# Attention into a GELU MLP on one core: four added exps per key in the first and last pair, products with v ahead of the sums, the last store in parts

## The chip, the cores and the metric

The kernel runs on one core of a Trainium2 chip. A core has five engines with instruction queues of their own: TensorE (PE; its weight loads are a row of their own, PEld), VectorE (DVE), ScalarE (ACT), GpSimd (POOL) and SyncE (SP, which here only issues DMAs). The metric is the device time of one execution in microseconds (us), and lower is better.

## The reference

Attention with normed queries and keys over 8 batches of 12 heads, 448 tokens and 64 channels; the heads are put side by side, and the 3584 tokens of 768 channels go through an MLP of width 2048:

```
q_n, k_n = rmsnorm(q, g_q), rmsnorm(k, g_k)
scores = matmul(q_n, k_n.T) / sqrt(64)
attn   = exp(scores - max); attn = attn / (sum(attn) + 1e-9)
x      = concat_heads(matmul(attn, v))          # 3584 x 768
out    = gelu_tanh(x @ w_in) @ w_out            # 768 -> 2048 -> 768
```

## The kernel before

**Work of one batch.** Batches are counted from 0 to 7. The twelve heads of a batch are six pairs (`hp` 0 to 5). The 448 keys stand in four key tiles of 112 (`kt`). `scores` (L208) multiplies one key tile of a pair with all queries: two matmuls, one per head, on separate halves of TensorE's rows, into a PSUM tile `sc` of which there are two; ScalarE takes the exp of both heads in one instruction (L218) into `ex`. `key_sums` (L222) lets VectorE add key tiles 0 and 1, then 2 and 3, into `es` (two additions per pair, batches 2 to 7 only; in batches 0 and 1 it returns). `pair_sums` (L231) is called twice per pair. With `what` 0 it sums over the keys: matmuls of `ones` with `es` (two key halves, two heads, so four matmuls) into the PSUM tile `o0`; then VectorE turns the sums into reciprocals that are spread over the channels: a transpose `st` (L253), a reciprocal `rc` (L254), a transpose `rb` (L255). With `what` 1 it multiplies `ex` with v (eight matmuls) into `o1`, and VectorE multiplies `o1` with `rb` into `xT` (L248). The two heads' matmuls stand in separate halves of TensorE's columns.

**Order of the work.** The order on every engine is written out by hand (`manual_schedule`, L62): each engine runs its instructions in the order of the Python code, and waits where data or a buffer is missing. The loop at L549 does for each batch b: the first MLP product `mm1` (L259; 16 tiles of six matmuls, each followed by a gelu on ScalarE), between whose tiles `m1` puts other work by slots; then `attention(b + 1)` (L334), between whose parts it puts the second MLP product `mm2` (L273) of earlier tokens: 112 steps of one matmul (96 in the first), given out by `upto`. Sixteen steps make half the columns of a tile of 128 tokens, and a copy by VectorE (L294) takes that out of PSUM; the PSUM tiles of `mm1` and `mm2` share a pool of two (`ps_m`). Within a pair the order on TensorE is: scores of key tiles 0 and 1, two steps of `mm2` in column halves, the previous pair's sums and products, scores of key tiles 2 and 3, nine or ten steps of `mm2`. The first pair has 20 and 30 as its counts (`first`), and ahead of and behind the last pair's sums stand 17 and 7 steps (`last`, L337).

**The next batches.** For batch b+1 GpSimd multiplies the loaded q and k with their inverse norms (L159, twelve instructions, slot 0 of `m1`), SP transposes them by DMA into `qT` and `kT` (L199), and VectorE multiplies `kT` with the gains (L204). For batch b+2 SP loads q and k (L96), ScalarE and, for the last third of the heads, GpSimd square them (L121, L123), and VectorE totals the squares (L128). The totals of that last third stand in slots 1 and 2 of the attention's `side`, on VectorE's queue between the first pair's two additions; the inverse norms are taken in slot 11 (L137, L140).

**The end.** Behind the last `mm1` stand 128 steps of `mm2`. Each tile of 128 tokens is stored when its second half is copied, in two DMAs on SP (L301), since its tokens cross a border of the output's layout. In this last stretch ScalarE copies the first halves (L292) and VectorE the second ones.

Of the kernel before, what the change touches and what calls it, by code (L numbers as in the profile page):

```python
# [8 lines left out]
F32 = mybir.dt.float32  # L9
BF16 = mybir.dt.bfloat16  # L10
# [6 lines left out]
def kernel(  # L17
# [11 lines left out]
    nc = tc.nc  # L29
    B, H, S, D = q.shape  # L30
    assert (B, H, S, D) == (8, 12, 448, 64)
    d_model = H * D
# [4 lines left out]
    HP = H // 2  # L37
# [87 lines left out]
    def total(b, c, n, hs=slice(0, CH)):  # L125
        if b not in sss:
            sss[b] = smp.tile([P, NCH, 2, CH, NK], F32, tag="ss", name="ss")
        nc.vector.reduce_sum(  # L128
            sss[b][:, c, "qk".index(n), hs], sqs[n, b, c][:, hs], axis=AX.X
        )  # L130
# [90 lines left out]

    def key_sums(b, hp, i):  # L222

        if b < 2:
            return
        if i == 0:
            ess[b, hp] = exq.tile([P, 2, 2, S], BF16, tag="es", name="es")
        ex = exs[b, hp]
        nc.vector.tensor_add(ess[b, hp][:, i], ex[:, 2 * i], ex[:, 2 * i + 1])  # L229

    def pair_sums(b, hp, what, waits=0):  # L231


        o = oas[what] = ps_o.tile([128, S], F32, tag=f"o{what}", name=f"o{what}")
        idle(waits, o)

        e = exs[b, hp] if what or b < 2 else ess[b, hp]
        n = e.shape[1]
        for i in range(n):
            for a in range(2):  # L240
                nc.tensor.matmul(  # L241
                    o[a * D:(a + 1) * D], vb[b % 2][:, 2 * hp + a, i] if what else ones, e[:, i, a],
                    start=(i == 0), stop=(i == n - 1),
                )
        if what:
            if hp == 0:
                xT[b] = xp.tile([128, HP, S], BF16, tag="xT", name="xT")
            nc.vector.tensor_mul(xT[b][:, hp], o, oas["rb"])  # L248
            return
        st = stp.tile([128, S // 32, 32], F32, tag="st", name="st")  # L250
        oas["rb"] = stp.tile([128, S], F32, tag="rb", name="rb")
        rc = smp.tile([128, S // 32], F32, tag="rc", name="rc")
        nc.vector.transpose(st.rearrange("p a b -> p (a b)"), o)  # L253
        nc.vector.reciprocal(rc, st[:, :, 0])  # L254
        nc.vector.transpose(oas["rb"], rc.to_broadcast([128, S // 32, 32]))  # L255

    hs1 = {}

# [14 lines left out]
    def mm2(b, i, half, f, parts=1):  # L273


        if f == 0:
            osbs["ps"] = ps_m.tile([128, 512], F32, tag="mm", name="o")
            if half == 0:
                osbs[i] = op.tile([128, d_model], F32, tag="osb", name="osb")
        o, osb = osbs["ps"], osbs[i]  # L280
        m = 128 // parts
        for j in range(parts):
            nc.tensor.matmul(  # L283
                o[j * m:(j + 1) * m, :HD], g[:, f, i * 128 + j * m:i * 128 + (j + 1) * m],
                wout[:, f, half * HD:(half + 1) * HD],
                start=(f == 0), stop=(f == nf - 1),
            )
        if f + 1 < nf:
            return
        part = osb[:, half * HD:(half + 1) * HD]  # L290
        if b + 1 == B and half == 0:
            nc.scalar.copy(part, o[:, :HD])  # L292
        else:
            nc.vector.tensor_copy(part, o[:, :HD])  # L294
        if half == 1:
            j = i * 128
            while j < (i + 1) * 128:
                bb, t, p = j // S, j % S // P, j % P
                m = min(P - p, (i + 1) * 128 - j)
                r = ((b // 2) * 2 + bb) * P + p  # L300
                nc.sync.dma_start(  # L301
                    out_v[t, r:r + m], osb[j - i * 128:j - i * 128 + m]
                )
                j += m

    def mm1_pair(i, cs=range(HP)):
# [27 lines left out]
    def attention(b, m2, quota, side):  # L334


        first, last, even = (20, 30), (17, 7), 2 if b > 1 else 0  # L337
        given = 0

        def upto(k, parts=1):  # L340
            nonlocal given
            while given < k:
                m2.pop(0)(parts)
                given += 1

        spread = quota - first[1] - sum(last)
        for hp in range(HP):
            for odd in range(2):
                i = 2 * hp + odd
                for fn in side.get(i, ()):  # L350
                    fn()
                if hp and not odd:
                    key_sums(b, hp - 1, 1)
                for kt in range(2 * odd, 2 * odd + 2):
                    scores(b, hp, kt)
                if not hp:
                    upto(first[odd])
                elif odd:
                    upto(first[1] + spread * hp // (HP - 1))
                else:  # L360

                    upto(given + even, 2)
                    for what in range(2):
                        pair_sums(b, hp - 1, what)
                if not odd:
                    key_sums(b, hp, 0)
        key_sums(b, HP - 1, 1)
        nc.scalar.preload_act_table_set(GELU_SET)
        upto(given + last[0])
        for what in range(2):  # L370
            pair_sums(b, HP - 1, what)
        upto(quota)

    def first_attention(side, mid, early, late):
# [128 lines left out]
    load_v(0, 6, 6)  # L503
    total(0, 1, "q", slice(0, 2))

    def pool_waits(b, c, n, j):

        nc.gpsimd.tensor_copy(mark, nrms[n, b, c][:1, j, 0, 0, :1])

    side = [(1, lambda: normed0(1, nc.vector), lambda: pool_waits(0, 0, "k", 1),  # L510
             lambda: squares0(3, nc.gpsimd), lambda: total(0, 1, "k", slice(0, 2)),
# [37 lines left out]
    for b in range(B):  # L549
        m1, side = [], []  # L550
        if b == 0:
            m1 = [(1, lambda: normed1(0), lambda: total(1, 1, "q"), lambda: total(1, 1, "k"),
                   lambda: load_v(1, CH, 2 * CH), lambda: rsqrt_pow(1, 1),
                   lambda: normed_all(1, 1)),
                  (2, lambda: total(1, 2, "q"), lambda: total(1, 2, "k"),
                   lambda: rsqrt_pow(1, 2), lambda: normed_all(1, 2)),
                  (3, lambda: trans(1, 0, ps_m)),
                  (4, lambda: trans(1, 1, ps_m), lambda: transposed(1, 1)),
                  (5, lambda: loads(2, 0), lambda: loads(2, 1)), (6, lambda: loads(2, 2))]
            side += [(0, lambda: transposed(1, 2)),  # L560
                     (2, lambda: gain(1, 1)), (5, lambda: gain(1, 2))]

            for c, slots in enumerate(((3, 5), (7, 9), (10, 11))):
                for n, slot in zip("qk", slots):
                    side += [(2 * c + 1, lambda c=c, n=n: square(2, c, n, nc.gpsimd)),
                             (slot, lambda c=c, n=n: total(2, c, n))]
        elif b + 1 < B:
            for c in range(NCH):
                m1 += [(0, lambda c=c: normed_all(b + 1, c)),
                       (4 * c + 4, lambda c=c: transposed(b + 1, c))]  # L570
            m1 += [(9, lambda: gain(b + 1, 0)), (14, lambda: gain(b + 1, 1))]
            side.append((3, lambda: gain(b + 1, 2)))
        if 0 < b and b + 2 < B:
            m1 += [(4, lambda: loads(b + 2, 1)), (8, lambda: loads(b + 2, 2))]
            for c, at in ((0, 1), (1, 9)):
                for i, (n, half) in enumerate((n, half) for n in "qk" for half in range(2)):
                    m1.append((at + i, lambda c=c, n=n, half=half: squared(b + 2, c, n, half)))
                m1 += [(at + 2, lambda c=c: total(b + 2, c, "q")),
                       (at + 4, lambda c=c: total(b + 2, c, "k"))]
            for n, slot in (("q", 1), ("k", 2)):  # L580
                m1.append((13, lambda n=n: square(b + 2, 2, n, nc.gpsimd)))
                side.append((slot, lambda n=n: total(b + 2, 2, n)))
        m1 = plan(*m1)
        for f in range(nf // 2 if b == 0 else nf):
            if b > 0:
                mm1(b, f)
            elif f > 1:
                mm1_pair(f)
            for fn in m1.get(f, ()):
                fn()  # L590
        m2 += m2_parts(b)
        if b + 1 == B:
            for fn in m2:
                fn()
            break
        nc.scalar.preload_act_table_set(EXP_SET)  # L596
        if b + 2 < B:
            side += [(11, lambda: rsqrt(b + 2)),
                     (0, lambda: load_v(b + 2, 0, H))]
            if b + 3 < B:  # L600
                side.append((1, lambda: loads(b + 3, 0)))
        attention(b + 1, m2, 96 if b == 0 else 112, plan(*side))


# [28 lines left out]
```

## Time and profile before

| what | value |
|---|---|
| median of 3 runs (lowest, highest) | 451.08 us (450.93, 451.17) |
| the profiled execution's own time | 451.04 us |
| span in its profile | 449.3 us |
| granted TensorE clock, mean | 0.996 |
| busy share: PE, ACT, DVE, POOL | 96%, 68%, 56%, 38% |
| one `mm1` of a batch, in the chain | 18.17 us |
| attention of batch 4, from its first scores to the next `mm1` | 217.83 to 251.05 us |
| start of the last copy; the last store's two issues on SP | 444.46; 445.09 to 445.87 us |

Times of single instructions are us from the start of the span. A timeline line gives the start, the stretch, engine, line, operation and how many instructions it merges; in brackets stands the idle time of the engine ahead of it and what ended that. A matmul's own duration (about 0.35 us) is longer than the distance to the next one, since matmuls overlap; distances between starts are used here. The profiled execution took 1.74 us more than its span, which no view splits up.

### The profile page before, as it was taken

The page shows a single profiled execution, that of the slowest core. Times are in us where ns is not written, and L with a number is a line of the kernel's source. Part 1 is how long each engine was busy: PE and PEld are TensorE (multiplying, and loading weights), DVE is VectorE, ACT ScalarE, POOL GpSimd, SP SyncE. Part 2 cuts the span into 40 slices and gives each one's busy share as a digit, 9 for nine tenths or more (in the row PEclk, how much of TensorE's full clock was granted, in tenths as well). Part 3 has the DMA queues.
Part 4 walks back from the last instruction along what each step waited for, and adds up shares of the span by engine and source line. Part 5 has one row for each costly group of instructions (what it writes and reads, how often), then busy time and mean ns, then how long its engine had stood idle before and what let it go on. Part 6 is the DMA issues. An engine that isn't in the chain of part 4 may idle for free.

```text
span 449.3 us, 7158 instructions
## 1 busy us (share of the span) xinstructions
PE 432.5 (96%) x2835; PEld 217.4 (48%) x2835; DVE 251.9 (56%) x426; ACT 303.7 (68%) x404; POOL 168.8 (38%) x142
## 2 busy tenths in 40 slices
PE   8889998899999999999999999999999999999995
PEld 3334543355445554455545544455544554545563
DVE  5889423943687428862588437872398513871000
ACT  5995477557787578857889468856888348863400
POOL 5997894573303740083402921064400900000000
PEclk9999999899999999999999999999999999999999
DMA  8999999159911939119911868118841511111022
GB/s 226 257 232 213 204 247 224 48 118 238 181 35 42 231 88 179 35 54 251 190 41 36 190 133 174 42 36 205 138 77 35 120 41 36 36 36 36 0 72 70
DMA packets 80754, 54.47 MB, mean 121 GB/s; under 512 B 39248, under 2 KB 75600, under 8 KB 80720
## 3 DMA queue, kind: packets, MB, share of 16 engines
q1 hardware_dynamic: 63936, 42.22, 38.5%
q0 software_dynamic: 16624, 11.80, 17.9%
q8 instruction: 22, 0.36, 0.3%
q14 instruction: 12, 0.10, 0.1%
q10 hardware_dynamic: 160, 0.00, 0.0%
HBM read 45.61 MB, written 11.01 MB: 126 GB/s over the span
## 4 chain that ended last, share of the span: by engine, by line
PE 70%; POOL 12%; DVE 7%; ACT 4%; DMA 4%; issue 2%; SPq 0%; DVEq 0%; POOLq 0%
PE h L262 28%; PE o L283 25%; PE o L241 10%; PE sc L214 7%; DVE ss L128 4%; POOL g L123 3%; POOL rinv L147 2%; DMA kT<-nrmk 2%; ACT ex L218 2%; POOL nrmk L159 2%; POOL nrmq L159 2%; ACT L596 1%; POOL sq L123 1%; DVE es L229 1%; DMA rawq<-in_q_dram 1%
## 5 line engine op out<-in xcount | busy, mean ns | idle before, releaser
L218 ACT ACTIVATE ex<-sc,shift 112x896 bf16<-112x896 f32 x192 | 182.7, 1004 | 27.9 <-PE sc L214 26.8
L283 PE MATMUL o<-wout,g 128*128 128x384 bf16 (+1 forms) x956 | 161.4, 328 | 0.6 <-DVE osb L294 0.6
L262 PE MATMUL h<-xT,win 128*128 128x448 bf16 x672 | 128.3, 352 | 0.0
L283 PEld LDWEIGHTS <-g 128*128 128x128 bf16 (+1 forms) x956 | 81.4, 99 | 70.9 <-issue 24.1
L266 ACT ACTIVATE g<-h 128x448 bf16<-128x448 f32 x112 | 61.0, 545 | 73.3 <-PE h L262 70.5
L262 PEld LDWEIGHTS <-win 128*128 128x128 bf16 x672 | 65.8, 98 | 61.0
L159 POOL TENSOR_TENSOR nrmq<-rawq,rinv 112x512 bf16<-112x512 f32 x44 | 46.9, 1083 | 126.8 <-issue 123.0
L128 DVE TENSOR_REDUCE ss<-sq 112x16 f32<-112x1024 f32 (+1 forms) x44 | 49.5, 1143 | 58.6 <-ACT sq L121 58.0
L294 DVE COPY osb<-o 128x384 f32<-128x384 f32 x52 | 28.6, 552 | 81.9 <-PE o L283 81.9
L214 PE MATMUL sc<-qT,kT 64*128 64x448 bf16 x384 | 57.3, 355 | 6.8 <-ACT ex L218 2.6
L229 DVE TENSOR_TENSOR es<-ex 112x896 bf16<-112x896 bf16 x72 | 47.7, 662 | 2.7 <-ACT ex L218 1.7
L159 POOL TENSOR_TENSOR nrmk<-rawk,rinv 112x512 bf16<-112x512 f32 x44 | 47.1, 1089 | 0.0
L241 PE MATMUL o<-ex,vb 112*64 112x448 bf16 x384 | 45.6, 357 | 0.6 <-DVE xT L248 0.6
L253 DVE STREAM_TRANSPOSE st<-o 128x448 f32<-128x448 f32 x48 | 31.1, 649 | 26.3 <-PE o L241 26.3
L214 PEld LDWEIGHTS <-kT 64*128 64x128 bf16 x384 | 17.4, 93 | 48.8 <-issue 40.3
L123 POOL TENSOR_TENSOR sq<-rawq 112x1024 f32<-112x1024 f32 x9 | 17.0, 1894 | 44.3 <-DVE ss L128 28.0
L248 DVE TENSOR_TENSOR xT<-o,rb 128x448 bf16<-128x448 f32 x48 | 30.0, 625 | 5.4 <-PE o L241 0.6
L255 DVE STREAM_TRANSPOSE rb<-rc 128x448 f32<-128x448 f32 x48 | 31.0, 645 | 1.6
L241 PEld LDWEIGHTS <-vb 112*64 112x64 bf16 x384 | 23.5, 110 | 12.8 <-issue 2.0
L123 POOL TENSOR_TENSOR sq<-rawk 112x1024 f32<-112x1024 f32 (+1 forms) x11 | 19.4, 1768 | 11.9 <-DVE ss L128 10.4
L241 PE MATMUL o<-es,ones 112*64 112x448 bf16 x144 | 22.3, 357 | 0.6
L241 PEld LDWEIGHTS <-ones 112*64 112x64 bf16 x240 | 15.2, 111 | 15.3 <-issue 9.2
(56 smaller groups left out, 219.7 us busy)
## 6 DMA issues: line engine op xcount, KB each, us to landing
rawq<-in_q_dram SPq DMA_DIRECT2D x22, 448.0 KB, 5.2
rawk<-in_k_dram SPq DMA_DIRECT2D x22, 448.0 KB, 6.3
vb<-in_v_dram POOLq DMA_DIRECT2D x6, 672.0 KB, 7.5
win<-in_moe_w_in_dram POOLq DMA_DIRECT2D x2, 1536.0 KB, 15.8
wout<-in_moe_w_out_dram POOLq DMA_DIRECT2D x2, 1536.0 KB, 19.0
out_dram<-osb SPq DMA_DIRECT2D x8, 336.0 KB, 2.8
out_dram<-osb SPq DMA_DIRECT2D x8, 288.0 KB, 2.7
out_dram<-osb SPq DMA_DIRECT2D x8, 240.0 KB, 2.7
```

Source lines behind the costliest of these rows:

```text
L123: eng.tensor_mul(sq, raw, raw)
L128: nc.vector.reduce_sum(sss[b][:, c, "qk".index(n), hs], sqs[n, b, c][:, hs], axis=AX.X)
L159: eng.tensor_mul(nrms[n, b, c][:, j].rearrange("p t a d -> p a t d"), raws[n, b, c][:, 2 * j:2 * j + 2], rinvs[b][:, c, "qk".index(n), 2 * ...
L214: nc.tensor.matmul(sc[:, a, :S], kT[r, hp, kt], qT[b][r, hp], start=True, stop=True,)
L218: nc.scalar.activation(exs[b, hp][:, kt], sc[:P, :, :S], AF.Exp, scale=scale, bias=shift)
L229: nc.vector.tensor_add(ess[b, hp][:, i], ex[:, 2 * i], ex[:, 2 * i + 1])
L241: nc.tensor.matmul(o[a * D:(a + 1) * D], vb[b % 2][:, 2 * hp + a, i] if what else ones, e[:, i, a], start=(i == 0), stop=(i == n - 1),)
L253: nc.vector.transpose(st.rearrange("p a b -> p (a b)"), o)
L255: nc.vector.transpose(oas["rb"], rc.to_broadcast([128, S // 32, 32]))
L262: nc.tensor.matmul(h[:, :S], win[:, c, f * 128:(f + 1) * 128], xT[b][:, c], start=(c == 0), stop=(c == HP - 1),)
L266: nc.scalar.activation(g[:, f, (b % 2) * S:(b % 2 + 1) * S], h[:, :S], AF.Gelu_apprx_tanh)
L283: nc.tensor.matmul(o[j * m:(j + 1) * m, :HD], g[:, f, i * 128 + j * m:i * 128 + (j + 1) * m], wout[:, f, half * HD:(half + 1) * HD], start ...
```

## The change

In batches 2 to 7 (`b > 1`):

- In the first and the last pair a third addition sums the two halves of `es` in place (`es[:, 0] += es[:, 1]`), and the sum over keys takes two matmuls and not four.
- In all pairs the eight products with v come ahead of the matmuls with `ones`; `st`, `rc`, `rb` and the multiplication into `xT` follow both.
- Around the last pair's products stand 12 and 12 steps of `mm2` (17 and 7 before).
- The two totals of batch b+2's last third are put in slot 0 of the attention, ahead of the first pair's additions on VectorE's queue (slots 1 and 2 before). This holds for all batches that have them.
- In the iterations of batches 2 to 6, GpSimd copies one element of the last pair's `es` ahead of the norms of the next batch, and so waits for the last addition.

And at the end of the kernel the last tile's first half of columns is stored alone once ScalarE has copied it; of the second half ScalarE copies 192 columns and stores them in two DMAs on its own queue, VectorE copies the other 192 into a tile `fin` that SP stores in two DMAs.

```diff
     def key_sums(b, hp, i):
...
-        ex = exs[b, hp]
-        nc.vector.tensor_add(ess[b, hp][:, i], ex[:, 2 * i], ex[:, 2 * i + 1])
-
-    def pair_sums(b, hp, what, waits=0):
+        ex, es = exs[b, hp], ess[b, hp]
+        nc.vector.tensor_add(es[:, i], ex[:, 2 * i], ex[:, 2 * i + 1])
+        if i == 1 and hp in (0, HP - 1):
+            nc.vector.tensor_add(es[:, 0], es[:, 0], es[:, 1])
+
+    def pair_products(b, hp, what, waits=0):
...
-        n = e.shape[1]
+        n = 1 if not what and b > 1 and hp in (0, HP - 1) else e.shape[1]
...
+    def pair_ends(b, hp):
+
+        for what in (1, 0) if b > 1 else (0, 1):
+            pair_products(b, hp, what)
+        pair_recips()
+        pair_x(b, hp)
...
         part = osb[:, half * HD:(half + 1) * HD]
-        if b + 1 == B and half == 0:
+        end = b + 1 == B and i + 1 == 2 * S // 128
+        if end:
+            ends = [(osb, slice(half * HD, (half + 1) * HD), nc.sync)]
+            if half == 0:
+                nc.scalar.copy(part, o[:, :HD])
+            else:
+                n = HD // 2
+                fin = op.tile([128, d_model], F32, tag="osb", name="fin")[:, :n]
+                nc.scalar.copy(part[:, :n], o[:, :n])
+                nc.vector.tensor_copy(fin, o[:, n:HD])
+                ends = [(osb, slice(HD, HD + n), nc.scalar),
+                        (fin, slice(HD + n, d_model), nc.sync)]
+        elif b + 1 == B and half == 0:
...
-        first, last, even = (20, 30), (17, 7), 2 if b > 1 else 0
+        first, last, even = (20, 30), (12, 12) if b > 1 else (17, 7), 2 if b > 1 else 0
...
-                    for what in range(2):
-                        pair_sums(b, hp - 1, what)
+                    pair_ends(b, hp - 1)
...
-        for what in range(2):
-            pair_sums(b, HP - 1, what)
+        pair_ends(b, HP - 1)
         upto(quota)
...
+    def gpsimd_waits(x):
+
+        nc.gpsimd.tensor_copy(mark, x)
...
         elif b + 1 < B:
+            if b > 1:
+
+                m1.append((0, lambda: gpsimd_waits(ess[b, HP - 1][:1, 0, 0, :1])))
             for c in range(NCH):
...
-            for n, slot in (("q", 1), ("k", 2)):
+            for n in "qk":
                 m1.append((13, lambda n=n: square(b + 2, 2, n, nc.gpsimd)))
-                side.append((slot, lambda n=n: total(b + 2, 2, n)))
+                side.append((0, lambda n=n: total(b + 2, 2, n)))
```

`pair_recips` holds the old L250 to L255 and `pair_x` the old L246 to L248, unchanged.

More of the change, by code (lines that the diff above doesn't have):

```diff
@@ L244, in pair_sums, with pair_recips @@
                 )
[L245 to L249, printed above, removed]
+    def pair_recips():
         st = stp.tile([128, S // 32, 32], F32, tag="st", name="st")
@@ L252, in pair_sums, with pair_x @@
         rc = smp.tile([128, S // 32], F32, tag="rc", name="rc")
-        nc.vector.transpose(st.rearrange("p a b -> p (a b)"), o)
+        nc.vector.transpose(st.rearrange("p a b -> p (a b)"), oas[0])
         nc.vector.reciprocal(rc, st[:, :, 0])
         nc.vector.transpose(oas["rb"], rc.to_broadcast([128, S // 32, 32]))
+    def pair_x(b, hp):
+        if hp == 0:
+            xT[b] = xp.tile([128, HP, S], BF16, tag="xT", name="xT")
+        nc.vector.tensor_mul(xT[b][:, hp], oas[1], oas["rb"])
+    def pair_sums(b, hp, what, waits=0):
+        pair_products(b, hp, what, waits)
+        if what:
+            pair_x(b, hp)
[4 more added lines that the diff above has]
+            pair_products(b, hp, what)
+        pair_recips()
+        pair_x(b, hp)
     hs1 = {}
@@ L290, in mm2 @@
         part = osb[:, half * HD:(half + 1) * HD]
-        if b + 1 == B and half == 0:
+        end = b + 1 == B and i + 1 == 2 * S // 128
[3 more added lines that the diff above has]
+                nc.scalar.copy(part, o[:, :HD])
+            else:
+                n = HD // 2
[5 more added lines that the diff above has]
+        elif b + 1 == B and half == 0:
             nc.scalar.copy(part, o[:, :HD])
@@ L294, in mm2 @@
             nc.vector.tensor_copy(part, o[:, :HD])
-        if half == 1:
+        if half == 1 or end:
+            if not end:
+                ends = [(osb, slice(0, d_model), nc.sync)]
             j = i * 128
@@ L300, in mm2 @@
                 r = ((b // 2) * 2 + bb) * P + p
-                nc.sync.dma_start(
-                    out_v[t, r:r + m], osb[j - i * 128:j - i * 128 + m]
-                )
+                for src, cols, eng in ends:
+                    own = src[j - i * 128:j - i * 128 + m]
+                    eng.dma_start(out_v[t, r:r + m, cols], own[:, cols] if src is osb else own)
                 j += m
@@ L504 @@
     total(0, 1, "q", slice(0, 2))
+    def gpsimd_waits(x):
+        nc.gpsimd.tensor_copy(mark, x)
     def pool_waits(b, c, n, j):
-        nc.gpsimd.tensor_copy(mark, nrms[n, b, c][:1, j, 0, 0, :1])
+        gpsimd_waits(nrms[n, b, c][:1, j, 0, 0, :1])
     side = [(1, lambda: normed0(1, nc.vector), lambda: pool_waits(0, 0, "k", 1),
```

## The prediction

> **What bounds the kernel now.** First the page's busy shares and its chain of work:
>
> ```profile
> PE 432.5 (96%) x2835; PEld 217.4 (48%) x2835; DVE 251.9 (56%) x426; ACT 303.7 (68%) x404; POOL 168.8 (38%) x142
> PE 70%; POOL 12%; DVE 7%; ACT 4%; DMA 4%; issue 2%; SPq 0%; DVEq 0%; POOLq 0%
> ```
>
> TensorE carries 70% of the chain, and the POOL part lies in the first 80 us, which the change leaves alone. Within the batches that it touches the question is how much TensorE works and how often it stands still. That shows in TensorE's timeline of batch 4's attention (217.83 to 251.05, 33.22 us). The distance from one line's start to the next one's is what a group costs:
>
> ```profile
> 223.89 0.55 PE L214 MATMUL sc<-qT,kT 64*128 64x448 bf16 x4
> 224.37 0.52 PE L283 MATMUL o<-wout,g 128*64 128x384 bf16 x4
> 224.72 0.86 PE L241 MATMUL o<-es,ones 112*64 112x448 bf16 x4
> 225.39 0.95 PE L241 MATMUL o<-ex,vb 112*64 112x448 bf16 x8
> 226.27 0.55 PE L214 MATMUL sc<-qT,kT 64*128 64x448 bf16 x4
> 226.75 1.64 PE L283 MATMUL o<-wout,g 128*128 128x384 bf16 x9
> 228.32 0.68 PE L214 MATMUL sc<-qT,kT 64*128 64x448 bf16 x4
> 228.93 0.52 PE L283 MATMUL o<-wout,g 128*64 128x384 bf16 x4
> 229.28 0.55 PE L241 MATMUL o<-es,ones 112*64 112x448 bf16 x4
> 229.66 0.92 PE L241 MATMUL o<-ex,vb 112*64 112x448 bf16 x8
> ```
>
> The four sums of pair 1 cost 0.38 (229.28 to 229.66), so one key half (two heads side by side) costs 0.19. Pair 0's cost 0.67: 0.29 of standing still. Scores cost 0.48 (223.89 to 224.37), but 0.61 at 228.32: 0.13 lost. Such losses, each group against its undisturbed kind, add up to 0.84 us in this attention; the rest is work without a gap. What pair 0 waits for stands in VectorE's timeline:
>
> ```profile
> 221.73 0.63 DVE L229 TENSOR_TENSOR es<-ex 112x896 bf16<-112x896 bf16 x1
> 222.27 2.34 DVE L128 TENSOR_REDUCE ss<-sq 112x16 f32<-112x1024 f32 x2
> 224.53 0.62 DVE L229 TENSOR_TENSOR es<-ex 112x896 bf16<-112x896 bf16 x1
> ```
>
> The two totals stand between the additions; the second addition ends at 225.15, and the second key half's matmul starts at 225.20. In batch 7, which has no totals, pair 0's sums cost 0.38 and the attention takes 33.00 (372.25 to 405.25).
>
> **Pair 0, walked forward (batch 4's times).** Scores of pair 1's key tiles 0 and 1 at 223.89 as now; +0.48 and +0.35 (two half-column steps) puts the products with v at 224.72. Four key tiles at 0.19 are 0.75: sums at 225.47, one key half 0.19, and 0.10 for the change to scores (0.85 for x8 less 0.75): the next scores at 225.76, not 226.27. Do the sums have to wait? The totals are gone from between, so the second addition starts behind the exp that ends at 223.99 (222.08 + 1.91), at 224.02; the third starts 0.54 later (221.73 to 222.27) and ends at 225.18: 0.24 of room. The in-place sum has no row; its bounds are 0.45 (the gain L204, 896 bf16 elements too, one input) and 0.99 (an addition beside GpSimd); I take 0.62, that of its nearest kin, the first two. At 0.99 it would wait 0.13.
>
> The 0.51 isn't all won. There are two `sc` tiles, so key tile 3's scores need the exp of key tile 1 done, and this ends at 226.20 (224.29 + 1.91) whatever TensorE does. Key tile 3 starts at 226.25, not at 225.96, against 226.47 now: a gain of 0.22 with a new wait of 0.29. Then nine steps as now: pair 2's second scores tile at 228.30 instead of 228.63, since the wait of 0.13 falls away (its exp now ends at 228.07). **Gain to here 0.35.**
>
> **Pairs 1 to 4** keep their number of instructions; the products go ahead of the sums. The sums come 0.75 later in a pair, and so does VectorE's `st`, while the additions that they wait for follow from the previous pair's `st`: that loop (st, rc, rb, xT, addition, copy, addition: 0.69 + 0.27 + 0.75 + 0.55 + 0.53 + 0.48 + 0.62 = 3.9, and 0.46 to the next `st`) stays at 4.36 with a copy against TensorE's 4.13 to 4.29 per pair, as now. `o1` is free in time: `xT` ends 0.7 ahead of the next products. I leave the remaining waits of these pairs (0.42 in batch 4) as they are: cost 0, bounds -0.3 (they vanish) to +0.3.
>
> **Last pair.** One key half less: **0.19**. 12 + 12 steps of `mm2` are as many as 17 + 7, so they cost nothing more; they shift the sums. The sums come at 248.64 - 5 x 0.163 + 0.75 - 0.35 = 248.2. The additions: without norms beside them 0.62 each; the first starts 0.4 later than 245.16 (as `st` does, 0.75 less 0.35), then the copy, then two at 0.54 apart: the third ends near 247.8, 0.4 ahead. Behind the sums VectorE needs 0.39 + 1.71 + 0.62 = 2.72 until `xT` is whole; the next `mm1` wants it in its sixth matmul, 0.29 + 12 x 0.163 + 0.95 = 3.19 later. The closest is the copy that VectorE has queued behind `xT`: it frees the PSUM tile of `mm1`'s second tile, 0.39 + 2.26 + 0.55 = 3.20 behind the sums, wanted after 2.24 + 1.135 = 3.38. Now the room there is 0.13 (252.06 to 252.19); it stays about that.
>
> **GpSimd's wait.** Why it is there shows where the norms run beside the additions (one line is GpSimd's):
>
> ```profile
> 244.52 2.42 POOL L159 TENSOR_TENSOR nrmq<-rawq,rinv 112x512 bf16<-112x512 f32 x2 [24.63 <-issue]
> 245.16 0.88 DVE L229 TENSOR_TENSOR es<-ex 112x896 bf16<-112x896 bf16 x1
> 246.43 0.99 DVE L229 TENSOR_TENSOR es<-ex 112x896 bf16<-112x896 bf16 x1
> ```
>
> 0.88 and 0.99 instead of 0.62, and 2.42 for two norms instead of 2.04. The norms now start near 247.9, 3.3 later, and win 0.8 back. Queued behind them on GpSimd: the squares at 266.18, which have waited 8.85 us for VectorE. On SP: six transposes, and behind each of the first two pairs of them the loads of batch b+2. The norms of the first third end near 251.9, so SP's loads move from 251.54 to about 253.3 and those of 256.93 to about 258.7; at 5.2 to landing that is 263.9, ahead of the squares. In the odd batches SP stands behind a store until 304.4 anyhow. Cost 0. The cover goes if the squares end over 3.3 us later (270.43 to 273.7): then the totals, now ahead of the first addition, hold up pair 0, one us per us in four batches.
>
> **Per batch:** 0.35 + 0.19 = 0.54 in batches 2 to 6. Batch 7 has no totals to move; there 33.00 becomes the same 33.22 - 0.54 = 32.68: 0.32. Sum 5 x 0.54 + 0.32 = **3.0**.
>
> **The last store.** Now:
>
> ```profile
> 444.46 0.56 DVE L294 COPY osb<-o 128x384 f32<-128x384 f32 x1 [4.70 <-PE o L283]
> 445.09 0.78 SPq L301 DMA_DIRECT2D out_dram<-osb  x2
> ```
>
> The second issue starts at 445.45 and lands at about 448.25. A copy of 192 columns has no row; between 0.24 (VectorE's 14 columns, L254) and 0.56 I take 0.39 by the straight line, and for ScalarE 0.28 (line from 0.48 at 384 and 1.0 at 896): 0.16 earlier. Landing took 2.8 for 336 KB (112 tokens whole) and 1.7 to 1.8 for 48 to 96 KB in this stretch. The two queues move 168 KB in their large parts, half of it each: 1.84 to 2.16 on the line of these rows. ScalarE issues slower than SP (0.55 and 0.61 at the start, 0.32 and 0.41 on SP), so its second issue starts 0.2 later than SP's. Together 0.6 to 1.0 saved; I take **0.75**. Bounds: -0.3 (four DMAs of short pieces land later) to 1.1.
>
> The Trainium skill speaks against part of this: DMA: Bandwidth & Descriptors, "Anatomy of one DMA", puts a constant of about 2.0 us on a DMA, most of it the receipt of the last write, and only bytes / 436 GB/s on top (fitted there for GpSimd's DMAs). By that 336 KB take 2.8, as the row has it, but 168 KB still 2.4, so my estimate from that page is 0.16 + 0.4 = 0.55 for the store, and 447.5 us in all.
>
> **Sum:** 451.04 (the profiled execution: span 449.3 and 1.74 around it, unchanged) - 3.0 - 0.75 = **447.3 us**. The median, 451.08, is 0.04 above it.
>
> **Rivals.**
> - *TensorE gets all of pair 0.* The new wait of 0.29 for the exp doesn't show, because the exps move up with the scores ahead of them. For it: exps are as a rule released by scores (26.8 us in the waits). Against: the scores at 223.89 don't move. Another 6 x 0.3 = 1.8: **445.5**. Chance 0.12.
> - *ScalarE becomes the bound.* From 226.67 four exps run with 0.9 to 0.95 between starts, nearly without a gap; if its chain through the two `sc` tiles eats pair 0's gain wherever the work gets denser, only the last pair's 6 x 0.19 and half the store stay: **449.5**. Against: ScalarE stands idle 0.2 to 0.3 ahead of most pairs of exps. Chance 0.15.
> - *The third addition is slow* (0.99 to 1.4 in place), and both sums wait for it, 0.3 to 0.5 a batch: **450.4**, within 0.2% of now. Chance 0.05.
> - *Slower: the norms moved onto VectorE's last chain.* They now begin just as `st`, `rc`, `rb`, `xT` and the copy are due. If each of these five lost the 0.37 that the addition lost, the chain would be 1.85 longer; 0.13 is hidden, so 1.7 a batch in batches 2 to 6, less 0.54: 5 x 1.16 - 0.32 - 0.75 = +4.7, **455.8**. It eats the gain from about 0.9 of lengthening on. Against: at 249.25 to 252.06 the same five run beside norms now, in 0.65, 0.24, 0.65, 0.62 and 0.55 as elsewhere. Chance 0.06 for this and anything else that ends slower.
>
> **Chances.** The forecast has 0.62 (own range 446.5 to 448.2). A measurement of this kernel tells about 0.2% (0.9 us) from no change. Faster by over 0.2%: 0.62 + 0.12 + 0.15 = 0.89; within 0.2%: 0.05; slower: 0.06. The range goes from the first rival to the second, 445.3 to 449.6.
>
> **What would show it.** Matmuls of `ones` with `es` x120, not x144; pair 0's sums without a wait, a wait of about 0.3 at the scores behind them; from one `mm1` to the next 50.9 us, not 51.47 (148.27 to 199.74 in the chain); the last additions at 0.62 and norms at 2.04; the squares still started by VectorE's totals; the last store landing 0.6 to 1.0 us nearer to the last matmul. It is wrong if pair 0's scores wait longer, if `mm1`'s first tiles wait for VectorE, or if the totals end behind the first exps.

## The result and the profile after

The changed kernel takes 446.94 us in the median of 4 runs (445.79 to 447.63), the kernel before beside it 451.0 (449.99 to 451.17): a ratio of 0.9912 with a 95% interval of 0.9885 to 0.9939. It is faster, by 2.7 to 5.2 us.

| distance in the trace, us | before | after |
|---|---|---|
| start of batch 1's `mm1` | 96.63 | 96.94 |
| from one `mm1` to the next, five times (batches 1 to 6) | 51.47 | 50.92 |
| the same from batch 6 to batch 7 | 51.25 | 50.92 |
| start of the last `mm1` to the end of the span | 44.02 | 43.41 |
| span; time of the profiled execution | 449.27; 451.04 | 445.85; 447.63 |

The two traces differ by 3.42 us: five times 0.55 and once 0.33 are 3.1 in the batches, 0.61 is the end, and 0.31 went the other way ahead of batch 2, where nothing was changed (the last section says from what). Busy shares and chain of the page after:

```profile
PE 430.7 (97%) x2811; PEld 215.0 (48%) x2811; DVE 255.2 (57%) x438; ACT 303.4 (68%) x405; POOL 170.2 (38%) x147
...
PE 78%; POOL 11%; DMA 3%; ACT 3%; DVE 2%; issue 2%; ACTq 0%; POOLq 0%; DVEq 0%
```

24 matmuls are gone (2835 to 2811), DVE's share of the chain falls from 7% to 2%, and TensorE's rises to 78%. Some 1.5 of DVE's 5 points belong to the first 97 us, which the change leaves alone; nearly all of the rest are the totals and additions of batches 2 to 6. TensorE's timeline of batch 4's pair 0, in the same order as the lines of before:

```profile
223.09 0.55 PE L214 MATMUL sc<-qT,kT 64*128 64x448 bf16 x4
223.57 0.52 PE L303 MATMUL o<-wout,g 128*64 128x384 bf16 x4
223.92 0.93 PE L244 MATMUL o<-ex,vb 112*64 112x448 bf16 x8
224.68 0.35 PE L244 MATMUL o<-es,ones 112*64 112x448 bf16 x2
224.97 0.85 PE L214 MATMUL sc<-qT,kT 64*128 64x448 bf16 x4
225.75 1.64 PE L303 MATMUL o<-wout,g 128*128 128x384 bf16 x9
227.32 0.55 PE L214 MATMUL sc<-qT,kT 64*128 64x448 bf16 x4
227.80 0.52 PE L303 MATMUL o<-wout,g 128*64 128x384 bf16 x4
```

The products follow the half-column steps, the sums are two matmuls and follow after 0.76 without a wait. The scores behind them cost 0.78 (224.97 to 225.75) and not 0.48. What the 0.30 wait for, the chain of the same stretch shows in order of time (start, us, what):

```profile
223.15 0.32 PE sc L214 x2
223.47 0.02 issue
223.49 1.91 ACT ex L218 x2
225.41 0.04 issue
225.45 0.36 PE sc L214 x2
```

Between the first and the second scores of pair 1 the path leaves TensorE and runs through two exps of ScalarE. VectorE in the same batch, pair 0's additions and the last pair's:

```profile
220.93 0.63 DVE L230 TENSOR_TENSOR es<-ex 112x896 bf16<-112x896 bf16 x1
223.21 0.62 DVE L230 TENSOR_TENSOR es<-ex 112x896 bf16<-112x896 bf16 x1 [1.66 <-ACT ex L218]
223.87 0.62 DVE L232 TENSOR_TENSOR es<-es 112x896 bf16<-112x896 bf16 x1
...
245.68 0.62 DVE L230 TENSOR_TENSOR es<-ex 112x896 bf16<-112x896 bf16 x1
246.33 0.62 DVE L232 TENSOR_TENSOR es<-es 112x896 bf16<-112x896 bf16 x1
```

All take 0.62 or 0.63: the totals have gone from between them, and GpSimd is silent beside the last pair's (0.88 and 0.99 before). GpSimd's timeline shows its copy, 28.00 idle us behind its last work (before, the norms started after 24.63), and the norms behind it at 2.04 for two:

```profile
247.09 0.18 POOL L541 COPY mark<-es 1x1 bf16<-1x1 bf16 x1 [28.00 <-DVE es L232]
247.23 2.04 POOL L159 TENSOR_TENSOR nrmq<-rawq,rinv 112x512 bf16<-112x512 f32 x2
```

And the end of the kernel on all engines:

```profile
441.60 0.32 ACT L320 COPY osb<-o 128x192 f32<-128x192 f32 x1 [2.08 <-PE o L303]
441.95 0.83 ACTq L338 DMA_DIRECT2D out_dram<-osb  x2
441.95 0.36 DVE L321 COPY fin<-o 128x192 f32<-128x192 f32 x1 [4.99 <-ACT osb L320]
442.34 0.78 SPq L338 DMA_DIRECT2D out_dram<-fin  x2
```

VectorE's copy doesn't run beside ScalarE's: it waits for it and starts 0.35 later. Why the program makes it wait no run shows.

### The profile page after: what moved, and what is told of

The parts are those of the page before. It is cut to its first block, busy times and chain, and to the rows that moved or that the text cites. A ratio compares the mean times of both kernels' runs of the same rounds, so it can differ in the third digit from the quotient of the medians.

```text
span 445.9 us, 7102 instructions
## 1 busy us (share of the span) xinstructions
PE 430.7 (97%) x2811; PEld 215.0 (48%) x2811; DVE 255.2 (57%) x438; ACT 303.4 (68%) x405; POOL 170.2 (38%) x147
## 4 chain that ended last, share of the span: by engine, by line
PE 78%; POOL 11%; DMA 3%; ACT 3%; DVE 2%; issue 2%; ACTq 0%; POOLq 0%; DVEq 0%
PE o L303 32%; PE h L282 29%; PE o L244 9%; PE sc L214 9%; ACT ex L218 3%; POOL rinv L147 2%; POOL g L123 2%; DMA kT<-nrmk 2%; POOL nrmk L159 2%; POOL nrmq L159 2%; POOL sq L123 2%; DMA grow<-in_g_k_dram 1%; POOL vb L112 1%; POOL wout L501 1%; POOL win L495 0%
## 5 line engine op out<-in xcount | busy, mean ns | idle before, releaser
L214 PE MATMUL sc<-qT,kT 64*128 64x448 bf16 x384 | 59.2, 359 | 6.3 <-ACT ex L218 2.6
L541 POOL COPY mark<-es 1x1 bf16<-1x1 bf16 x5 | 0.9, 177 | 138.1 <-DVE es L232 138.1
L230 DVE TENSOR_TENSOR es<-ex 112x896 bf16<-112x896 bf16 x72 | 44.0, 617 | 9.5 <-ACT ex L218 9.3
L159 POOL TENSOR_TENSOR nrmk<-rawk,rinv 112x512 bf16<-112x512 f32 x44 | 48.8, 1127 | 0.0
L159 POOL TENSOR_TENSOR nrmq<-rawq,rinv 112x512 bf16<-112x512 f32 x44 | 44.9, 1037 | 5.3 <-ACT rinv L140 4.9
L123 POOL TENSOR_TENSOR sq<-rawq 112x1024 f32<-112x1024 f32 x9 | 18.0, 1995 | 29.0 <-DVE ss L128 15.5
L244 PEld LDWEIGHTS <-vb 112*64 112x64 bf16 x384 | 21.1, 110 | 15.8 <-issue 4.3
L349 PE MATMUL hh<-xT,win 128*128 128x448 bf16 x96 | 18.8, 352 | 0.2 <-DVE xT L261 0.2
```

The lines of the kernel that those rows point to most:

```text
L123: eng.tensor_mul(sq, raw, raw)
L159: eng.tensor_mul(nrms[n, b, c][:, j].rearrange("p t a d -> p a t d"), raws[n, b, c][:, 2 * j:2 * j + 2], rinvs[b][:, c, "qk".index(n), 2 * ...
L214: nc.tensor.matmul(sc[:, a, :S], kT[r, hp, kt], qT[b][r, hp], start=True, stop=True,)
L230: nc.vector.tensor_add(es[:, i], ex[:, 2 * i], ex[:, 2 * i + 1])
L244: nc.tensor.matmul(o[a * D:(a + 1) * D], vb[b % 2][:, 2 * hp + a, i] if what else ones, e[:, i, a], start=(i == 0), stop=(i == n - 1),)
```

## The experiments

Whole times spread by 1 to 2 us between executions, but the distance from one `mm1` to the next agrees within 0.02 us inside every trace (five or six batches). So the verdicts rest on that distance ("per batch": 51.47 before, 50.92 after), and on the stretch from the last `mm1` to the end (44.02 and 43.41). The expectation ahead of each run gives the number of its theory. All edits but those of the two kernels named at the end are made to the changed kernel.

### The totals back between pair 0's additions

```diff
-            for n in "qk":
+            for n, slot in (("q", 1), ("k", 2)):
...
-                side.append((0, lambda n=n: total(b + 2, 2, n)))
+                side.append((slot, lambda n=n: total(b + 2, 2, n)))
```

> The changed kernel with the two totals back in slots 1 and 2, between the first pair's additions. Measure: the distance from one mm1 to the next for the attentions of batches 3 to 6 (50.92 us in the changed kernel, 51.47 before). Theory (ScalarE's exps pace pair 0 next to TensorE): with the products first the sums would wait about 0.3 us for the third addition, but TensorE would have stood still for the exp of key tile 1 there anyway, so most of it is free: 51.0 to 51.1. Rival (the move of the totals is the gain): the 0.3 us come back in full, with the third addition behind them 0.5: 51.2 to 51.45.

Measured: 51.04 per batch, 0.12 more than 50.92; batch 7, without totals, keeps 50.92. In batch 4 the sums come 1.14 behind the products, with VectorE's third addition named as what ended the wait, where after the change they come 0.76 behind them:

```profile
222.74 0.93 PE L244 MATMUL o<-ex,vb 112*64 112x448 bf16 x8
223.88 0.38 PE L244 MATMUL o<-es,ones 112*64 112x448 bf16 x2 [0.21 <-DVE es L232]
```

But the scores behind them cost 0.48 (224.19 to 224.67) and no longer 0.78. One wait of 0.38 has taken the place of the other of 0.30, and 0.26 of the 0.38 are free. The rival, that the move of the totals is the whole gain of pair 0, is out.

### The third addition in the last pair only

```diff
-        if i == 1 and hp in (0, HP - 1):
+        if i == 1 and hp == HP - 1:
...
-        n = 1 if not what and b > 1 and hp in (0, HP - 1) else e.shape[1]
+        n = 1 if not what and b > 1 and hp == HP - 1 else e.shape[1]
```

> The changed kernel with the third addition in the last pair only; the first pair's sums take four matmuls again. Theory: TensorE's 0.19 us less in pair 0 is worth nothing, as key tile 3's scores wait for an exp that ends at the same time: 50.92 to 50.96 per batch, with the wait at those scores about 0.1 and not 0.3. Rival (TensorE's work decides): 51.11 per batch.

Measured: 50.92 per batch, the same to 0.01. Pair 0 does 0.19 us more on TensorE, and the scores behind it cost 0.59 (225.64 to 226.23) instead of 0.78. The third addition of the first pair is worth nothing. That of the last pair was not taken out in any run; for its 0.19 there is only the distance of before and after, given below.

### One exp made shorter

Of pair 1's key tile 1 in batches 2 to 7 ScalarE takes the exp of one head only (m = 1), and GpSimd writes ones in the other head's place: this kernel leaves out a part of the computation.

```diff
+        m = 1 if b > 1 and hp == 1 and kt == 1 else 2
+        if m == 1:
+            nc.gpsimd.memset(exs[b, hp][:, kt, 1], 1.0)
         nc.scalar.activation(
-            exs[b, hp][:, kt], sc[:P, :, :S], AF.Exp, scale=scale, bias=shift
+            exs[b, hp][:, kt, :m], sc[:P, :m, :S], AF.Exp, scale=scale, bias=shift
         )
```

> The changed kernel, but of pair 1's key tile 1 in batches 2 to 7 ScalarE takes the exp of one head only (GpSimd fills the other head's place with ones, so that part of the computation is left out): this one exp takes about 0.55 us, not 1.0. Theory: the wait of 0.30 at pair 1's second scores is a wait for this exp and goes; the scores behind them then wait 0.1 more, so the batch gains 0.15 to 0.3: 50.6 to 50.75. Rival (the wait comes from something else, such as the change between matmul forms): 50.92 and the wait stays at 0.3.

Measured: 50.68 per batch, 0.24 less. The scores in question now cost 0.48 (TensorE's timeline, batch 4):

```profile
223.41 0.55 PE L214 MATMUL sc<-qT,kT 64*128 64x448 bf16 x4
223.89 1.64 PE L306 MATMUL o<-wout,g 128*128 128x384 bf16 x9
```

The next ones cost 0.60 (225.46 to 226.06), 0.12 more than 0.48, as expected. So the new wait is one for that exp, which is shown here and not only read from the chain.

### GpSimd's wait taken out

```diff
             if b > 1:
 
-                m1.append((0, lambda: gpsimd_waits(ess[b, HP - 1][:1, 0, 0, :1])))
+                pass
```

> The changed kernel without GpSimd's wait, so that the norms run beside the last pair's additions. Theory: the three additions take 0.9 to 1.0 us each, the third ends about 1 us later than now with 0.3 to 0.4 of room, and the copy behind xT frees the PSUM tile for mm1's second tile too late: 0.4 to 0.7 more per batch in batches 2 to 6, 51.3 to 51.6. Rival (the additions are off the path, the wait does nothing): 50.92. Second rival (the wait costs, since everything behind the norms comes later): under 50.9.

Measured: 52.19 per batch in the five batches, 1.27 more than with the wait and 0.72 more than before the change; the run took 455.01 us beside 449.92 for the kernel before. Both rivals are out. The theory had the slowed additions, but neither the place where TensorE pays nor the price: it expected a wait at `mm1`'s second tile, and `mm1` takes 17.97 from its first to its last matmul, with the wait and without. VectorE's timeline, and TensorE's, of batch 4:

```profile
248.26 1.18 DVE L230 TENSOR_TENSOR es<-ex 112x896 bf16<-112x896 bf16 x1
249.37 0.54 DVE L327 COPY osb<-o 128x384 f32<-128x384 f32 x1
249.83 0.99 DVE L230 TENSOR_TENSOR es<-ex 112x896 bf16<-112x896 bf16 x1
250.86 1.35 DVE L232 TENSOR_TENSOR es<-es 112x896 bf16<-112x896 bf16 x1
```

```profile
249.96 0.81 PE L303 MATMUL o<-wout,g 128*128 128x384 bf16 x4 [0.31 <-DVE osb L327]
250.70 0.95 PE L244 MATMUL o<-ex,vb 112*64 112x448 bf16 x8
252.26 0.38 PE L244 MATMUL o<-es,ones 112*64 112x448 bf16 x2 [0.61 <-DVE es L232]
```

The additions take 1.18, 0.99 and 1.35, 1.66 more than three times 0.62. TensorE pays at two places: a step of `mm2` waits for the copy that stands on VectorE's queue between the additions (18 steps from 246.56 should end the stretch at 249.49; the next starts at 249.96: 0.47), and the sums come 1.56 and not 0.78 behind the products (0.78). Together 1.25 of the 1.27. The copy between the additions was not in the theory.

### The sums ahead of the products

```diff
-        for what in (1, 0) if b > 1 else (0, 1):
+        for what in (0, 1):
```

> The changed kernel with the sums ahead of the products with v again, all else as changed. Theory: pair 0's sums are due 0.75 us earlier and wait 0.5 us for the third addition; part of that takes the place of the wait for the exp: 51.2 to 51.35 per batch. Rival (the order alone is free, since the same matmuls run): 50.92.

Measured: 51.43 per batch, 0.51 more, above the theory's 51.2 to 51.35. Pair 0's sums start 0.98 behind the half-column steps and not 0.35: a wait of 0.63. The room was counted too large: the third addition needs the result of the second one and starts 0.66 behind it (223.83 to 224.49), not 0.54 as an independent one does (two in a row take 1.15 at 240.33 in the changed kernel, 0.61 of it the second). Of the 0.63 the 0.30 for the exp falls away (those scores cost 0.49, 226.24 to 226.73), and 0.12 come back at pair 2's second scores (228.30 to 228.90: 0.60, not 0.48): 0.45 of the 0.51. The last pair, 6.70 from its steps to `mm1`, loses nothing. With three additions in the first pair, the old order gives 0.51 of the 0.55 back.

### 17 and 7 steps around the last pair

```diff
-        first, last, even = (20, 30), (12, 12) if b > 1 else (17, 7), 2 if b > 1 else 0
+        first, last, even = (20, 30), (17, 7), 2 if b > 1 else 0
```

> The changed kernel with 17 and 7 steps of mm2 around the last pair instead of 12 and 12. TensorE's work is the same. Theory: with products first, VectorE's chain behind the sums (0.39 + 1.71 + 0.62 to xT, 3.20 to the end of the copy) finds only 2.4 and 2.6 us of work as cover: mm1 loses 0.4 us at its sixth matmul and 0.3 at its second tile, 51.6 per batch, for batch 7 too. Rival (the place of the steps is free): 50.92.

Measured: 51.53 per batch from batch 2 on, 0.61 more; the time goes inside `mm1`, which takes 18.58 from its first to its last matmul and not 17.97. In batch 4 its sixth matmul starts at 252.24 and not at 251.90, 0.05 behind the end of `xT` (251.56 + 0.63): 0.33 lost; its second tile starts at 252.70, 0.46 and not 0.19 later, 0.05 behind the copy (252.10 + 0.55): 0.28 lost. Both waits are those of the theory. The steps cost the same wherever they stand, but with the sums at the end of the pair seven of them no longer cover VectorE's chain.

### The last store as before

```diff
-        end = b + 1 == B and i + 1 == 2 * S // 128
+        end = False
```

> The changed kernel with the last tile stored whole as before. Per batch 50.92. From the start of the last copy to the end of the span 4.80 us as before the change, against 4.27 in the changed kernel: 0.5 us more in all. Rival: the parts gain nothing, 4.3 here too.

Measured: 50.92 per batch; from the last copy to the end 4.83; from the last `mm1` to the end 44.05, 0.64 more than 43.41. The parts of the store gain 0.6 us.

### One engine copies both parts

```diff
-                nc.scalar.copy(part[:, :n], o[:, :n])
+                nc.vector.tensor_copy(part[:, :n], o[:, :n])
                 nc.vector.tensor_copy(fin, o[:, n:HD])
```

> The changed kernel with VectorE making both copies of the last half tile, one behind the other. In the changed kernel VectorE's copy started only when ScalarE's had ended (441.95 behind 441.60 + 0.32), so the two did not run beside each other. Theory: two copies by one engine cost the same as two that wait for each other; from the start of the first copy to the end of the span 4.2 to 4.4 us, as in the changed kernel (4.27). Rival (the second engine helps): 4.6 or more.

Measured: VectorE's copies start at 441.96 and 442.23, and 4.15 pass from the first one to the end, against 4.25 in the changed kernel (441.60 to 445.85); from the last `mm1` 43.36. The second copying engine brings nothing. What the two queues and the smaller pieces bring was not tried apart.

### The larger piece first

A tile's tokens go out in two pieces; in the changed kernel's last tile 16 tokens are issued ahead of 112.

```diff
-            while j < (i + 1) * 128:
+            for j, m in pieces[::-1] if end else pieces:
...
                 for src, cols, eng in ends:
```

> The changed kernel, with the larger of each part's two pieces of the last tile (112 tokens) stored ahead of the smaller one (16 tokens). Theory: of two issues the second one starts about 0.37 us later and sets the landing; with the small piece there, the last write comes 0.1 to 0.4 us earlier: from the start of the last mm1 to the end of the span 43.0 to 43.3, not 43.41, and 50.92 per batch as before. Rival (the constant part of a landing decides): 43.4.

Measured: 50.92 per batch, 43.25 from the last `mm1` to the end: 0.16 less than the changed kernel, where the traces with the changed store as it is have 43.40 to 43.41 (six of them; the 17 and 7 steps have 44.01, 0.61 of it inside `mm1`). The whole time is 446.61 us in the median of 4 runs (445.83 to 447.75), ratio 0.9927 with an interval of 0.9904 to 0.995 to the kernel before. It is faster than the kernel before; the 0.16 against the changed kernel shows only in the one trace, since the whole times of the two kernels overlap.

### The totals alone, in the kernel before

```diff
-            for n, slot in (("q", 1), ("k", 2)):
+            for n in "qk":
...
-                side.append((slot, lambda n=n: total(b + 2, 2, n)))
+                side.append((0, lambda n=n: total(b + 2, 2, n)))
```

> The kernel before with one part of the change alone: the two totals in slot 0, ahead of the first pair's additions. Theory: pair 0's sums wait no longer (0.29 us), and like batch 7, which has no totals, the batches come to 51.25 to 51.3 per batch, 0.2 less than 51.47, since the exp of key tile 1 takes over 0.1 of it. Rival (all of the 0.29 is won): 51.18.

Measured: 51.25 per batch in all batches, batch 7's distance of before. This part alone brings 0.22 of the 0.55, and 0.12 in the changed kernel (first experiment): the parts share what they win.

### GpSimd's wait alone, in the kernel before

```diff
         elif b + 1 < B:
+            if b > 1:
+                m1.append((0, lambda: nc.gpsimd.tensor_copy(mark, ess[b, HP - 1][:1, 1, 0, :1])))
```

> The kernel before with GpSimd's wait alone (for the second addition of the last pair's sums). Theory: without the third addition and with 17 steps ahead of the sums, the slowed additions were hidden; they come back to 0.62 us and the norms start some 2.5 us later, and nothing of either shows: 51.47 per batch. Rival (the wait is a gain by itself): under 51.4. Second rival (later norms cost): over 51.5.

Measured: 51.46 per batch, 51.25 to batch 7: nothing. The additions do fall from 0.88 and 0.99 to 0.61 and 0.63, and the norms start behind them, and neither shows. The wait is worth 1.27 us a batch only in the changed kernel, where the third addition, the later sums and the 12 steps together have used up the room; which of the three does it was not tried apart.

## Why the prediction was right

**Pair 0, 0.35 forecast.** From the first scores of pair 1 to the half-column steps behind pair 2's first ones (223.89 to 228.93 before, 223.09 to 227.80 after) it is 5.04 and 4.71: 0.33. The wait for the exp, forecast at 0.29, is 0.30. The shorter exp confirms the mechanism, and the third addition in the last pair only confirms its consequence, that TensorE's 0.19 less is not won here. The room for the third addition was given as 0.24 and was about 0.12 less, since an addition that reads the one before it starts 0.66 and not 0.54 behind it; it held.

**Pairs 1 to 4, cost 0.** From there to the `mm2` steps behind the last scores it is 15.22 and 15.18: 0.04 won.

**Last pair, 0.19.** TensorE's lines of batch 4, before and then after:

```profile
244.15 4.56 PE L283 MATMUL o<-wout,g 128*128 128x384 bf16 x27
248.64 0.57 PE L241 MATMUL o<-es,ones 112*64 112x448 bf16 x4
249.04 0.92 PE L241 MATMUL o<-ex,vb 112*64 112x448 bf16 x8
249.90 1.31 PE L283 MATMUL o<-wout,g 128*128 128x384 bf16 x7
251.05 5.27 PE L262 MATMUL h<-xT,win 128*128 128x448 bf16 x27
```

```profile
242.98 3.75 PE L303 MATMUL o<-wout,g 128*128 128x384 bf16 x22
246.66 0.95 PE L244 MATMUL o<-ex,vb 112*64 112x448 bf16 x8
247.44 0.36 PE L244 MATMUL o<-es,ones 112*64 112x448 bf16 x2
247.73 2.12 PE L303 MATMUL o<-wout,g 128*128 128x384 bf16 x12
249.69 0.54 PE L282 MATMUL h<-xT,win 128*128 128x448 bf16 x2
```

From its steps to `mm1` 6.90 and 6.71: 0.19. That the cover of 3.19 to 3.38 us is near its limit shows in the 17 and 7 steps: 5 x 0.163 = 0.8 of it taken away cost 0.61.

**GpSimd's wait, cost 0.** Right: where the wait stands, the squares, loads and totals behind it came in time. The prediction gave no price for leaving it out; it is 1.27 a batch. One of the signs of being wrong did show, ahead of the first of these waits: in batch 2 the second total ended at 119.43, behind the first two exps (117.16 + 1.90), because its squares had waited for a load. It moved the first addition by 0.7 and cost nothing (50.92), since the second one waits for a later exp.

**Sum of the batches, 3.0:** 3.1.

**The store, 0.75:** 0.61. This is the term that was mis-sized. That it still came within its 0.6 to 1.0 is partly luck: the copies and the end of the program lost time that it had not counted, and the landing gained nearly the most that it allowed.

- The copies were to run side by side and end 0.16 earlier. They run one behind the other: VectorE's ends at 442.31, 0.71 behind the start of the first, where the single copy of before took 0.56. SP's last issue starts 1.10 behind the start of the first copy (442.70), before 0.99 (445.45): 0.11 lost. That last issue is SP's, not ScalarE's (442.35) as forecast.
- From that issue to its landing, the semaphore that tells of it, it is 1.85 (444.55) and before 2.78 (448.23): 0.93 gained, where the forecast had 0.64 to 0.96.
- Behind the landing 1.30 pass to the end of the span, before 1.04: 0.26 lost that the forecast had at nothing. By the trace's records of SP, it waits there for one semaphore after another, 0.06 us apart, and has six left behind the last landing (to 444.96), where it had two (to 448.40). With the larger piece first, and with one copier, the same stretch is 1.30 and 1.29; with the store as before it is 1.05.

The first copy also starts 0.05 earlier behind the last `mm1`: 0.05 - 0.11 + 0.93 - 0.26 = 0.61. The second estimate in the prediction, 0.55, came out nearer, but by luck: it had 0.4 for the landing, which gained 0.93, and the copies 0.16 earlier. It rests on the constant of about 2.0 us that the Trainium skill (DMA: Bandwidth & Descriptors, "Anatomy of one DMA") puts on a DMA, fitted there for GpSimd's; this case's stores by SP differ, since the one that landed last took 1.85 in all.

**The whole time.** Forecast 447.3, median 446.94. The four runs of the changed kernel spread over 1.84 us, so that the 0.4 between the two numbers says little; the better test is the gain in the trace behind the start of batch 1's `mm1`, 3.75 forecast and 3.7 measured.

**Rivals.** That TensorE gets all of pair 0 is out: the exps behind pair 1's first scores start 0.40 behind them as before (224.29 behind 223.89, 223.49 behind 223.09). ScalarE did become the bound, but for 0.30 in one pair, not for all of its gain. The third addition wasn't slow beside a silent GpSimd (0.62; 1.35 beside a busy one). The norms moved onto VectorE's last chain left it at 0.65, 0.24, 0.65 and 0.63, as the rows of before had it.

**Slips without weight.** Pair 0's 0.35 is 0.33 by the prediction's own times (228.63 to 228.30). The four exps from 226.67 do not all start 0.9 to 0.95 apart: the third starts 1.15 behind the second (227.58 to 228.73). And six batches at 0.3 to 0.5 make the third rival 449.1 to 450.3, not 450.4.

## What to carry to other kernels

Work taken from the bounding engine counts only up to the next wait in the same stretch: walk the stretch forward with each engine's spacings, and ask of every buffer whether its reader has ended, before counting what was removed. An edit that uses up the room of one engine makes an unrelated neighbour matter: here the same one-element wait is worth nothing in the one kernel and 1.27 us a batch in the other. And where times of whole runs spread, compare a distance that repeats inside the trace: here it agreed within 0.02 us, where whole times of one kernel lay up to 2 us apart.

## What the runs showed of the hardware

**The first 97 us differ by a landing and by the granted clock.** The spread between executions lies ahead of the changed code: `mm1` of batch 1 starts at 95.22 to 97.96 in the thirteen traces. Two things move it. VectorE's multiplication of `kT` with the gains (L204), which waits for a DMA there, starts at 77.09 to 79.24. And soon behind it the granted TensorE clock falls to 0.50, for 3.41 us in six of the traces (80.45 to 83.86 before the change) and for 6.83 us in the other seven (80.97 to 87.80 after it); as a mean from 72 to 95 us that is 0.93 and 0.85. From 100 us to 440 us it is 1.00 in all. From the multiplication to `mm1` it is 18.12 or 18.13 in the six and 18.56 to 19.33 in the seven. Of the two traces compared here, that of before has the short fall of the clock (18.12) but the later start (78.51), that of after the long one (19.33) and 77.61: 1.21 less 0.90 are the 0.31 that went the other way. The rows of this stretch, first before, then after the change (us, busy us and counts of PE, PEld, DVE, ACT and POOL, clock, DMA share, GB/s):

```profile
72.00:95.00 23.00, 18.78 (x129) 8.80 (x129) 14.13 (x23) 13.31 (x16) 8.12 (x7) 0.93 0.53 101
```

```profile
72.00:95.00 23.00, 19.81 (x128) 8.70 (x128) 14.31 (x22) 13.16 (x16) 7.96 (x7) 0.85 0.48 103
```

Both lengths occur among the variants of either kernel, whose edits don't touch this stretch. That the longer fall lengthens it is read from this split and was not tried apart, nor why the clock falls there.

**An addition beside GpSimd's norms** took 0.88 to 1.35 us instead of 0.62, and two norms 2.42 to 2.80 instead of 2.04. The multiplication and the transposes of VectorE, which read PSUM or a single tile of SBUF, kept their 0.62 to 0.65 beside the same norms. The Trainium skill (SBUF — State Buffer, "SBUF: two separate sides") has VectorE and GpSimd share one pair of ports, held for a whole instruction, when VectorE reads two SBUF inputs or runs in a two-port mode; this case agrees as far as it goes: the additions, with two SBUF inputs, are slowed, the others are not, and the largest loss, 0.73 on one addition, is less than one norm of 1.04. That the ports are held for a whole instruction no run here shows by itself.
